# An attention-and-MLP kernel whose main loop is moved to row halves of the TensorE array

## The chip, the cores and the metric

The kernel runs on one core of a Trainium2 chip. The metric is device time in microseconds. Engines are named as in the profile: PE is TensorE (PEld its weight loads), DVE VectorE, ACT ScalarE, POOL GpSimd, SP SyncE, which issues the DMAs here.

## The reference, cut to what matters

```python
# q, k, v: (4, 12480, 128); agents: (4, 49, 128); w_in: (128, 2048); w_out: (2048, 128)
agent_v = softmax(agents @ k.T / sqrt(128)) @ v     # per batch, 49 x 128
x       = softmax(q @ agents.T / sqrt(128)) @ agent_v
h       = x @ w_in
g       = h - tanh(h)
out     = g @ w_out
```

All is float32. The kernel folds `agent_v @ w_in` into one matrix of 49 x 2048 per batch (`aw`), so that `h` is the product of the 49 softmax weights of a token with `aw`. The values of `h` are small, and `h - tanh(h)` is taken as h * tanh(sqrt(0.6) h)^2 / 1.8; a general path for larger values lies behind a branch that is not taken here.

## The kernel before

Tokens are worked on in blocks of 500 (25 per batch, 100 in all), the 2048 columns in 8 pairs of 128-column chunks. A step `(n, i)` is one block and one pair of chunks: 800 steps. Two blocks (16 steps) are a double block; `pos` is the step's place in it, 0 to 15. PE multiplies in one pass with a rounded type (`F32R`); to keep precision each operand is split into a high and a low part. A step does this:

- `first_product` / `m1`, two steps ahead: `h` = (`awh` + `awl`) times `pT`. `pT` has 98 rows: 49 of high parts and 49 of low ones, and `aw` stands twice above itself. So each chunk takes two matmuls, four per pair (L537, L538). `h` lies in two PSUM banks.
- `tanhs` and `squares` on ACT, one step ahead: `y` (L546), `z` (L551).
- `product` on DVE: `g` = h * z (L556, `mul`); then on POOL `gh` = `g` rounded (L589, `high`); then, a step later, DVE takes `gl` = g - gh (L594, `low`).
- `out` / `m2`: six matmuls per pair add `gh` and `gl` times the parts of `w_out` to `acc`, one PSUM bank (L606, L607, L609). In the pair `PLAIN_PAIR` (7) of every second block, and in the whole first block, `g` is not split: two f32 matmuls with `wo_f` take its place, which PE runs in two passes each (L603).

When a block is done, ACT copies `acc` into `o` with the scale `GSC` (L770), and SP writes two blocks at once (L773). Beside this, the generators in `live` advance once a step. `q_softmax` makes the weights of the next double block: 32 small matmuls in column quarters (L494), maximum, exponential, sum, then `pp`, high and low parts beside each other. `q_transpose` brings `pp` into `pT` by PE (L524) and a copy on ACT (L529). `phase1(b + 1)` does the softmax over k for the next batch: `scores` (L277), maxima, `av` (L336), and `project` makes its `aw`. In the last batch there is none of it. The PSUM has eight banks: the pool `ph` with three pairs (`h`), `pmisc` with two single ones for all else.

On each engine the order is the order in the code (`issue_order`); the tables `KS`, `VS`, `OS`, `T0`, `T1`, `QGAPS` say at which `pos` the side jobs start and how many steps lie between their parts.

Of the kernel before, what the change touches and what calls it, by code (L numbers as in the profile page):

```python
# [30 lines left out]
NCH = FF // 128  # L31
TT = 126
# [9 lines left out]
GW = 2 * BLK  # L42
NBLK = -(-N // BLK)
# [6 lines left out]
GSC = 1.0 / (3.0 * 0.6)  # L50
# [7 lines left out]
PLAIN_PAIR = NCH // 2 - 1  # L58
PLAIN_EVERY = 2
# [8 lines left out]
T0 = 12  # L68
T1 = 14
KS = (3, 5, 14)  # L70
VS = (1, 3, 12)
OS = (3, 5)
# [26 lines left out]
class Build:  # L99
    def __init__(self, ctx, tc, aps):  # L100
        self.tc, self.nc = tc, tc.nc
        self.qT, self.kT, self.v, self.agT, self.wi, self.wo, self.outT = aps
        self.pool = lambda name, bufs=1, **kw: tc.tile_pool(name=name, bufs=bufs, **kw)
        self.const = ctx.enter_context(self.pool("const"))
        self.keep = ctx.enter_context(self.pool("keep"))
        self.small = ctx.enter_context(self.pool("small", 2))
        self.ph = ctx.enter_context(self.pool("ph", 3, space=PSUM))
        self.pmisc = ctx.enter_context(self.pool("pmisc", 2, space=PSUM))
# [6 lines left out]

    def misc(self):
        return self.pmisc.tile([128, 512], F32, tag="misc", name="misc")

    def constants(self):
# [18 lines left out]
        self.wo_f = c.tile([128, 2, C], F32, tag="wo_f", name="wo_f")  # L138
        self.vb = [c.tile([128, GT, C + 2], F32, tag=f"v{i}", name=f"v{i}") for i in range(VB)]
        self.avs = c.tile([128, B, A2], F32, tag="avs", name="avs")  # L140
# [43 lines left out]
    def split_w_out(self, c):  # L184
# [7 lines left out]
        if c == PLAIN_PAIR // 2:  # L192
            nc.scalar.copy(self.wo_f.rearrange("p n e -> p (n e)"), w[:, 2 * C * (PLAIN_PAIR % 2) :][:, : 2 * C])

    def phase1(self, b):
# [36 lines left out]
        def scores(g):  # L232
            yield
            yield
# [8 lines left out]
            kt = ahead("k", load_k, g, 1 if b == 0 else kb - 1)  # L243
            if b and g >= NG - vb:
                ahead("v", load_v, 0, g - NG + vb + 1)
            if b == 0:
                ps = self.ph.tile([128, 2, 512], F32, tag="h", name="h")
# [65 lines left out]
        def av(g):  # L313
# [10 lines left out]
            yield  # L324
            if b:
                yield
                yield
            nc.scalar.activation(e3, e3, AF.Exp, scale=SCALE)
            yield
# [21 lines left out]
            if g == 0:  # L351
                ph = self.ph.tile([128, 2, 512], F32, tag="h", name="h")
                st["ps"], st["pr"] = ph[:, 0, :], ph[:, 1, :A]
# [33 lines left out]
        def sums():  # L387
# [6 lines left out]
            if b == 0:  # L394
# [8 lines left out]
                two = [128, 2, A]  # L403
                nc.vector.tensor_tensor(
                    self.avs[:, b, :].rearrange("p (two a) -> p two a", a=A),
                    pt[:, None, :A].broadcast_to(two),
                    sm[:, None, :].broadcast_to(two),
                    ALU.mult,
                )
# [11 lines left out]
            two = [128, 2, A]  # L421
            nc.vector.tensor_tensor(
                self.avs[:, b, :].rearrange("p (two a) -> p two a", a=A),
                pt[:, None, :A].broadcast_to(two),
                sm[:, None, :].broadcast_to(two),
                ALU.mult,
            )
# [5 lines left out]
        if b:  # L433
            jobs = [(KS, scores(g)) for g in range(NG)] + [(OS, max_in()), (OS, max_out())]
            jobs += [(VS, av(g)) for g in range(NG)]
            return jobs + [(OS, job) for job in [sums(), None] + self.project(b, True)]
# [3 lines left out]
    def project(self, b, bound):  # L440
        nc = self.nc

        def part(c, lo, hi):
            yield
            yield
            if c == 0:
                self.aw[b] = tuple(
# [4 lines left out]
            if b == 0 and bound and c < 2:  # L452
                ps = self.ph.tile([128, 2, 512], F32, tag="h", name="h")[:, 0, :]
            else:
                ps = self.misc()
            ps = ps[:A2, : hi - lo]
            nc.tensor.matmul(ps, self.avs[:, b, :], self.w_in[:, sl], start=True, stop=True)
            yield
            h = awh[:A2, sl]
# [3 lines left out]
            nc.vector.tensor_tensor(awl[:A2, sl], ps, h.bitcast(F32), ALU.subtract)  # L463
# [15 lines left out]
    def q_load(self, src):  # L479
        qt = self.keep.tile([128, GW], F32, tag="qt", name="qt", bufs=2)  # L480
# [3 lines left out]
    def q_softmax(self, halves, qt, res, TT=TT, gaps=(1,) * 7):  # L484
# [3 lines left out]
        for t in range(GT):  # L488
            b, at, w = halves[t // BT]
            at += min(t % BT * TT, w - TT)  # L490
            for r in range(0, TT, QUART):
                m = min(QUART, TT - r)
                to = ps[r : r + m, t * A : (t + 1) * A]
                nc.tensor.matmul(to, qt[:, at + r : at + r + m], self.ag[:, b, :], start=True, stop=True)  # L494
        yield from (None,) * gaps[1]
        pv = ps[:TT, : GT * A].rearrange("p (t a) -> p t a", a=A)
        m = self.small.tile([128, GT], F32, tag="qm", name="qm")
        e = self.small.tile([128, GT, A], F32, tag="qe", name="qe")
        ev = e[:TT]
        s = self.small.tile([128, GT], F32, tag="qs", name="qs")  # L500
        nc.vector.tensor_reduce(m[:TT], pv, axis=AX.X, op=ALU.max)
        nc.scalar.copy(ev, pv)  # L502
        yield from (None,) * gaps[2]
        nc.gpsimd.tensor_tensor(ev, ev, m[:TT, :, None].broadcast_to([TT, GT, A]), ALU.subtract)  # L504
# [3 lines left out]
        nc.vector.tensor_reduce(s[:TT], ev, axis=AX.X, op=ALU.add)  # L508
        nc.vector.tensor_scalar(s[:TT], s[:TT], EPS, None, ALU.add)
        nc.vector.reciprocal(s[:TT], s[:TT])  # L510
        nc.vector.tensor_tensor(ev, ev, s[:TT, :, None].broadcast_to([TT, GT, A]), ALU.mult)
        yield from (None,) * gaps[5]
        pp = self.small.tile([128, GT, A2], F32R, tag="pp", name="pp")
        (nc.scalar.copy if gaps[5] else nc.vector.tensor_copy)(pp[:TT, :, :A], ev)  # L514
        yield from (None,) * gaps[6]
        nc.gpsimd.tensor_tensor(pp[:TT, :, A:], ev, pp[:TT, :, :A].bitcast(F32), ALU.subtract)  # L516
        res.append(pp)

    def q_transpose(self, pp, half, res, w, TT=TT):
        nc = self.nc  # L520
        ps = self.misc()
        for t in range(BT):
            at = min(t * TT, w - TT)
            nc.tensor.transpose(  # L524
                ps[:A2, at : at + TT].bitcast(F32R), pp[:TT, half * BT + t, :], self.identr[:TT, :TT]
            )
        yield
        pT = self.keep.tile([128, BLK], F32R, tag="pT", name="pT", bufs=3)
        nc.scalar.copy(pT[:A2, :w], ps[:A2, :w])  # L529
        res.append(pT)  # L530

    def m1(self, aw, pT, i, w):
        nc = self.nc
        h = self.ph.tile([128, 2, 512], F32, tag="h", name="h")
        for c in range(2):
            sl = slice((2 * i + c) * 128, (2 * i + c + 1) * 128)
            nc.tensor.matmul(h[:, c, :w], aw[0][:A2, sl], pT[:A2, :w], start=True, stop=False)  # L537
            nc.tensor.matmul(h[:, c, :w], aw[1][:A2, sl], pT[:A2, :w], start=False, stop=True)  # L538
        return h[:, :, :w]

    def pair(self, t):
        return t.rearrange("p (c n) -> p c n", c=2)
# [6 lines left out]
    def square(self, y):  # L549
        z = self.wtile("z", NB["z"])[:, : y.shape[1]]  # L550
        self.nc.scalar.activation(z, y, AF.Square)  # L551
# [45 lines left out]
    def m2(self, acc, i, gh, gl, wf=None):  # L597
        nc = self.nc
        w = gh.shape[1] // 2
        parts = [(2 * i + c, slice(c * w, (c + 1) * w)) for c in range(2)]  # L600
        if gl is None:
            for c, (f, x) in enumerate(parts):
                nc.tensor.matmul(acc[:, :w], wf[:, c * C : (c + 1) * C], gh[:, x], start=f == 0, stop=f == NCH - 1)  # L603
            return
        for f, x in parts:
            nc.tensor.matmul(acc[:, :w], self.wo_l[:, f, :], gh[:, x], start=f == 0, stop=False)  # L606
            nc.tensor.matmul(acc[:, :w], self.wo_h[:, f, :], gh[:, x], start=False, stop=False)  # L607
        for f, x in parts:
# [326 lines left out]
```

## Time and profile before

| | |
|---|---|
| median of 3 runs | 2103.64 us (2102.35 to 2104.73) |
| the profiled execution | 2104.99 us, of it 2102.9 us span |
| granted TensorE clock | 0.996 |
| PE busy | 2072.6 us |
| DVE busy | 1958.9 us |
| ACT busy | 1796.8 us |
| POOL busy | 1409.8 us |
| first `g` of the main loop | at 60.12 us |

Busy time is the union of the recorded durations of an engine. Durations overlap where an engine pipelines: consecutive matmuls are recorded with 0.39 us each though they start 0.23 us apart, and a DVE operation of 1.19 us is followed after 1.11 us. Distances between starts therefore say what an operation occupies.

### The profile page before, as it was taken

What the parts mean: (1) busy time and instruction counts of PE and PEld (TensorE: products, weight loads), DVE (VectorE), ACT (ScalarE), POOL (GpSimd) and SP (SyncE); (2) the same over time, 40 slices, a digit from 0 to 9 for tenths busy, and PEclk for the clock granted to TensorE, in tenths of its full rate; (3) what the DMA queues carried; (4) which work ended last, traced back from release to release, by engine and by line L of the source; (5) the groups of instructions that cost most, each with busy time, mean ns of one, the idle gap of its engine ahead of it and who ended that gap; (6) DMA issues with size and microseconds to landing.
All of it is one profiled execution on the core that took longest, in us unless ns stands there. A gap on an engine that the chain in (4) does not pass through costs nothing.

```text
span 2102.9 us, 37664 instructions
## 1 busy us (share of the span) xinstructions
PE 2072.6 (99%) x14885; PEld 1642.1 (78%) x14885; DVE 1958.9 (93%) x2076; ACT 1796.8 (85%) x2088; POOL 1409.8 (67%) x857
## 2 busy tenths in 40 slices
PE   8899999999999999999999999999999999999998
PEld 7577777777777777877777777777777878878876
DVE  7899999999999999989999999999999999999998
ACT  3788889988888888998888888889888888888887
POOL 0366676667767676666677677667667777777776
PEclk9999999999999999999999999999999999999999
DMA  9222102210111121112002210121100000100000
GB/s 338 98 61 80 54 31 71 70 52 30 40 51 50 54 70 50 50 62 60 21 20 71 70 33 30 50 61 42 34 27 20 30 30 20 40 20 21 30 11 21
DMA packets 65353, 109.17 MB, mean 52 GB/s; under 512 B 3984, under 2 KB 44176, under 8 KB 65168
## 3 DMA queue, kind: packets, MB, share of 16 engines
q1 hardware_dynamic: 65168, 106.68, 15.5%
q8 instruction: 119, 1.95, 0.4%
q14 instruction: 66, 0.54, 0.1%
HBM read 81.10 MB, written 25.56 MB: 51 GB/s over the span
## 4 chain that ended last, share of the span: by engine, by line
PE 83%; DVE 11%; ACT 3%; issue 2%; POOL 1%; DMA 0%; POOLq 0%; SPq 0%; DVEq 0%; ACTq 0%
PE h L537 16%; PE h L538 15%; PE misc L609 15%; PE misc L606 14%; PE misc L607 14%; DVE g L556 4%; DVE gl L594 3%; PE misc L603 2%; PE misc L336 2%; PE misc L494 2%; PE h L249 1%; PE misc L524 1%; PE misc L277 1%; ACT z L551 1%; ACT y L546 1%
## 5 line engine op out<-in xcount | busy, mean ns | idle before, releaser
L589 POOL TENSOR_SCALAR gh<-g 128x1000 fp32r<-128x1000 f32 (+1 forms) x704 | 1230.8, 1748 | 347.0 <-DVE g L556 337.0
L556 DVE TENSOR_TENSOR g<-h,z 128x1000 f32<-128x1000 f32 (+1 forms) x800 | 951.2, 1192 | 102.3 <-ACT z L551 98.5
L546 ACT ACTIVATE y<-h 128x1000 f32<-128x1000 f32 (+1 forms) x800 | 805.0, 1006 | 225.9 <-PE h L538 220.5
L594 DVE TENSOR_TENSOR gl<-g,gh 128x1000 fp32r<-128x1000 f32 (+1 forms) x743 | 887.3, 1194 | 7.5 <-POOL gh L589 1.8
L551 ACT ACTIVATE z<-y 128x1000 f32<-128x1000 f32 (+1 forms) x800 | 833.8, 1042 | 17.5 <-DVE g L556 2.3
L537 PE MATMUL h<-pT,awh 98*128 98x500 f32 (+1 forms) x1600 | 668.7, 418 | 2.1 <-ACT awh L460 1.4
L538 PE MATMUL h<-pT,awl 98*128 98x500 f32 (+1 forms) x1600 | 622.3, 389 | 0.5 <-DVE awl L463 0.5
L606 PE MATMUL misc<-gh,wo_l 128*128 128x500 f32 (+1 forms) x1486 | 576.6, 388 | 0.5 <-POOL gh L589 0.5
L607 PE MATMUL misc<-gh,wo_h 128*128 128x500 f32 (+1 forms) x1486 | 575.0, 387 | 0.0
L609 PE MATMUL misc<-gl,wo_h 128*128 128x500 f32 (+1 forms) x1486 | 461.1, 391 | 10.8 <-DVE gl L594 9.5
L537 PEld LDWEIGHTS h<-pT,awh 98*128 98x128 f32 x1600 | 300.3, 188 | 85.8 <-issue 18.1
L538 PEld LDWEIGHTS h<-pT,awl 98*128 98x128 f32 x1600 | 302.2, 189 | 65.8 <-issue 13.6
L609 PEld LDWEIGHTS misc<-gl,wo_h 128*128 128x128 f32 x1486 | 274.0, 188 | 81.4 <-DVE gl L594 29.8
L606 PEld LDWEIGHTS misc<-gh,wo_l 128*128 128x128 f32 x1486 | 279.7, 188 | 59.7 <-POOL gh L589 3.3
L607 PEld LDWEIGHTS misc<-gh,wo_h 128*128 128x128 f32 x1486 | 280.8, 189 | 55.3
L516 POOL TENSOR_TENSOR pp<-qe,pp 126x392 fp32r<-126x392 f32 x50 | 49.1, 982 | 199.7 <-DVE pp L514 192.2
L504 POOL TENSOR_TENSOR qe<-qe,qm 126x392 f32<-126x392 f32 x50 | 55.2, 1105 | 111.5 <-ACT qe L502 111.5
L603 PE MATMUL misc<-g,wo_f 128*128 128x500 f32 (+1 forms) x196 | 90.1, 581 | 0.0
L321 POOL TENSOR_TENSOR s<-s,mb 128x392 f32<-128x392 f32 (+1 forms) x39 | 70.3, 1801 | 26.1 <-DVE g L556 26.1
L770 ACT ACTIVATE o<-misc 128x500 f32<-128x500 f32 (+1 forms) x100 | 58.0, 580 | 5.3 <-PE misc L609 5.3
L529 ACT CAST pT<-misc 98x500 fp32r<-98x500 f32 (+1 forms) x100 | 56.6, 567 | 1.8 <-PE misc L524 1.8
L603 PEld LDWEIGHTS misc<-g,wo_f 128*128 128x128 f32 x196 | 37.0, 189 | 26.3 <-issue 22.6
(105 smaller groups left out, 840.1 us busy)
## 6 DMA issues: line engine op xcount, KB each, us to landing
kt<-kT SPq DMA_DIRECT2D x48, 512.0 KB, 3.7
qt<-qT SPq DMA_DIRECT2D x46, 500.0 KB, 3.5
outT<-o SPq DMA_DIRECT2D x46, 500.0 KB, 2.6
v<-v SPq DMA_DIRECT2D x36, 512.0 KB, 4.1
vt<-v SPq DMA_DIRECT2D x12, 512.0 KB, 6.4
raw<-w_in SPq DMA_DIRECT2D x4, 512.0 KB, 9.3
v<-w_out SPq DMA_DIRECT2D x4, 512.0 KB, 8.2
qt<-qT SPq DMA_DIRECT2D x4, 490.0 KB, 3.4
```

The lines of the kernel that those rows point to most:

```text
L321: (nc.gpsimd if b else nc.vector).tensor_tensor(e3, sv, top, ALU.subtract)
L537: nc.tensor.matmul(h[:, c, :w], aw[0][:A2, sl], pT[:A2, :w], start=True, stop=False)
L538: nc.tensor.matmul(h[:, c, :w], aw[1][:A2, sl], pT[:A2, :w], start=False, stop=True)
L546: self.nc.scalar.activation(self.pair(y), h, AF.Tanh, scale=TSC)
L551: self.nc.scalar.activation(z, y, AF.Square)
L556: self.nc.vector.tensor_tensor(self.pair(g), h, self.pair(z), ALU.mult)
L589: self.nc.gpsimd.tensor_scalar(gh, g, 1.0, 0.0, ALU.mult, ALU.add)
L594: self.nc.vector.tensor_tensor(gl, g, gh.bitcast(F32), ALU.subtract)
L603: nc.tensor.matmul(acc[:, :w], wf[:, c * C : (c + 1) * C], gh[:, x], start=f == 0, stop=f == NCH - 1)
L606: nc.tensor.matmul(acc[:, :w], self.wo_l[:, f, :], gh[:, x], start=f == 0, stop=False)
L607: nc.tensor.matmul(acc[:, :w], self.wo_h[:, f, :], gh[:, x], start=False, stop=False)
L609: nc.tensor.matmul(acc[:, :w], self.wo_h[:, f, :], gl[:, x], start=False, stop=f == NCH - 1)
```

## The change

1. The array is used in two row halves. `aw` and `pT` stand at rows 0 to 48 and 64 to 112; a second tile `pb` holds `pT` with its parts exchanged, made by two DMAs. `m1` takes three products per chunk (low x high, high x high, high x low) of 49 rows each; the two chunks of a pair use the two halves, alternating, and two banks. Six half matmuls take the place of four whole ones.
2. `m2` takes each of its products in two halves of 64 rows, which add up in two banks of `acc`: twelve half matmuls for six. At a block's end ACT copies the one bank (`take`), and DVE adds the other (`add_up`). The scale goes into the Square of `z`.
3. f32 pairs stand at positions 3, 7 and 15 of a double block (`PLAIN`), where there was one at 7. (The short title of the change speaks of four; the code has three.)
4. One PSUM pool of four pairs of banks serves `h`, `acc`, the transposes (`pt`) and `misc`; two side jobs of one step can share a pair (`share`). In a step where a pair was lent out, and at `i == 2`, `first_product` stands behind `product` (`late`).
5. Transposes are half matmuls; tokens of a block are cut at 125 with halves of 63 and 62 that overlap, `h` has 504 columns, of which 500 are read. `pp` is one tile for all double blocks. The side jobs' positions are new.

```diff
-PLAIN_PAIR = NCH // 2 - 1
-PLAIN_EVERY = 2
+PLAIN = (3, 7, 15)
...
-T0 = 12
-T1 = 14
-KS = (3, 5, 14)
-VS = (1, 3, 12)
-OS = (3, 5)
+T0 = 11
+T1 = 15
+KS = {2: 1, 12: 2}
+VS = {15: 1, 9: 1, 11: 1}
+VGAPS = {15: (3, 1), 9: (3, 2), 11: (2, 1)}
+OS = {3: 1, 5: 1}
...
-        self.ph = ctx.enter_context(self.pool("ph", 3, space=PSUM))
-        self.pmisc = ctx.enter_context(self.pool("pmisc", 2, space=PSUM))
+        self.ph = ctx.enter_context(self.pool("ph", 4, space=PSUM))
...
+    def banks(self, name):
+        self.taken += 1
+        return self.ph.tile([128, 2, 512], F32, tag="h", name=name)
+
     def misc(self):
-        return self.pmisc.tile([128, 512], F32, tag="misc", name="misc")
+        if self.spare is not None:
+            ps, self.spare = self.spare, None
+            return ps
+        t = self.banks("misc")
+        if self.sharing:
+            self.spare = t[:, 1, :]
+        return t[:, 0, :]
...
+        pT, pb = (self.keep.tile([128, BT * TT], F32R, tag=t, name=t, bufs=2) for t in ("pT", "pb"))
...
+        nc.sync.dma_start(pb[HALF:PW].bitcast(F32), pT[:A].bitcast(F32))
+        nc.sync.dma_start(pb[:A].bitcast(F32), pT[HALF:PW].bitcast(F32))
...
     def m1(self, aw, pT, i, w):
+        h = self.banks("h")
+        rows = slice(0, A), slice(HALF, PW)
+        terms = (((1, 0), (0, 0)), ((0, 0), (1, 1)), ((0, 1), (0, 1)))
+        for k, both in enumerate(terms):
+            for c, (a, p) in enumerate(both):
+                sl = slice((2 * i + c) * 128, (2 * i + c + 1) * 128)
+                nc.tensor.matmul(
+                    h[:, c, : BT * TT], aw[a][rows[c], sl], pT[p][rows[c], :], start=k == 0, stop=k == 2
+                )
...
     def m2(self, acc, i, gh, gl, wf=None):
+            terms = [(low, gh, 0), (high, gh, 0), (low, gh, 1), (high, gh, 1), (high, gl, 0), (high, gl, 1)]
+        for k, (weights, g, c) in enumerate(terms):
+            for r in range(2):
+                rows = slice(HALF * r, HALF * (r + 1))
+                nc.tensor.matmul(
+                    acc[:, r, :w],
+                    weights(c)[rows],
+                    g[rows, c * w : (c + 1) * w],
...
+    def add_up(self, o, acc):
+        self.nc.vector.tensor_tensor(o, o, acc[:, 1, : o.shape[1]], ALU.add)
+
+    def take(self, o, acc):
+        self.nc.scalar.copy(o, acc[:, 0, : o.shape[1]])
...
             squares(k + 1)
-            first_product(k + AHEAD)
+            late = self.taken > taken or n and i == 2
+            if not late:
+                first_product(k + AHEAD)
...
             product(k, values)
+            if late:
+                first_product(k + AHEAD)
+            while done and done[0][1] < k - 1:
+                finish(done.pop(0)[0])
             low(1)
```

On PE, an f32 pair and the step after it in the last batch, before:

```order
L603 MATMUL misc<-g,wo_f 128x500 x2
L537 MATMUL h<-pT,awh 128x500
L538 MATMUL h<-pT,awl 128x500
L537 MATMUL h<-pT,awh 128x500
L538 MATMUL h<-pT,awl 128x500
L606 MATMUL misc<-gh,wo_l 128x500
L607 MATMUL misc<-gh,wo_h 128x500
L606 MATMUL misc<-gh,wo_l 128x500
L607 MATMUL misc<-gh,wo_h 128x500
L609 MATMUL misc<-gl,wo_h 128x500 x2
```

The same place now, `wo_f_86` being the f32 weights of one plain pair:

```order
L635 MATMUL acc<-g,wo_f_86 128x500 x4
L563 MATMUL h<-pT,awl 128x504
L563 MATMUL h<-pT,awh 128x504 x2
L563 MATMUL h<-pb,awl 128x504
L563 MATMUL h<-pb,awh 128x504 x2
L635 MATMUL acc<-gh,wo_l 128x500 x2
L635 MATMUL acc<-gh,wo_h 128x500 x2
L635 MATMUL acc<-gh,wo_l 128x500 x2
L635 MATMUL acc<-gh,wo_h 128x500 x2
L635 MATMUL acc<-gl,wo_h 128x500 x4
```

Six half matmuls stand for four whole ones in `m1`, twelve for six in `m2`, and every two neighbours use different halves.

On DVE, the steps around the maximum of the q scores (`qm`), early in a double block of the last batch, before:

```order
L556 TENSOR_TENSOR g<-h,z 128x1000
L594 TENSOR_TENSOR gl<-g,gh 128x1000
L556 TENSOR_TENSOR g<-h,z 128x1000
L594 TENSOR_TENSOR gl<-g,gh 128x1000
L501 TENSOR_REDUCE qm<-misc 126x8
L556 TENSOR_TENSOR g<-h,z 128x1000
L594 TENSOR_TENSOR gl<-g,gh 128x1000
```

And now:

```order
L583 TENSOR_TENSOR g<-h,z 128x1000
L644 TENSOR_TENSOR o<-o,acc 128x500
L621 TENSOR_TENSOR gl<-g,gh 128x1000
L583 TENSOR_TENSOR g<-h,z 128x1000
L621 TENSOR_TENSOR gl<-g,gh 128x1000
L514 TENSOR_REDUCE qm<-misc 128x8
L583 TENSOR_TENSOR g<-h,z 128x1000 x2
L621 TENSOR_TENSOR gl<-g,gh 128x1000
```

`add_up` (L644) has come in between `g` and `gl`, and the f32 pair at position 3 leaves two `g` in a row.

On SP, one double block of the last batch, before:

```order
L773 DMA outT<-o 128x1000
L481 DMA qt<-qT 128x1000
L773 DMA outT<-o 128x1000
L481 DMA qt<-qT 128x1000
L773 DMA outT<-o 128x1000
```

And now:

```order
L812 DMA outT<-o 128x1000
L495 DMA qt_98<-qT 128x1000
L551 DMA pb<-pT 49x504
L552 DMA pb<-pT 49x504
L551 DMA pb<-pT 49x504
L552 DMA pb<-pT 49x504
L812 DMA outT<-o 128x1000
```

Four transfers per double block have come in, each behind the copy of `pT` on ACT.

More of the change, by code (lines that the diff above doesn't have):

```diff
@@ L31 @@
 NCH = FF // 128
+PW = HALF + A
 TT = 126
@@ L42 @@
 GW = 2 * BLK
+QW = GW + 8
+TS = 128
 NBLK = -(-N // BLK)
@@ L806, in out @@
                 if i == 0:
-                    acc[n] = self.misc()
-                wf = self.wf[:, 2 * C * i :] if n == 0 else self.wo_f.rearrange("p c n -> p (c n)")
+                    acc[n] = self.banks("acc")
+                wf = self.wf[:, 2 * C * i :] if n == 0 else self.wo_f.get(i)
                 self.m2(acc[n], i, gh, gl, wf)
@@ L834, in fast @@
             nxt = []
+            taken = self.taken
+            self.share(True)
             for gen in live:
@@ L870, in fast @@
         while done:
+            self.take(out_at(done[0][0]), acc[done[0][0]])
             finish(done.pop(0)[0])
```

207 lines of the change are left out of this document (105 added, 102 removed).

## The prediction

> **What bounds the kernel now.** I read the page's busy times first, then the same by stage, then the chain and the waits, and last the timeline of one stretch. The busy times:
>
> ```profile
> PE 2072.6 (99%) x14885; PEld 1642.1 (78%) x14885; DVE 1958.9 (93%) x2076; ACT 1796.8 (85%) x2088; POOL 1409.8 (67%) x857
> PE 83%; DVE 11%; ACT 3%; issue 2%; POOL 1%; DMA 0%; POOLq 0%; SPq 0%; DVEq 0%; ACTq 0%
> ```
>
> The second line is the chain that ended last: PE holds 83% of it. The output transfers mark the double blocks (two blocks, 16 steps), one each:
>
> ```profile
> 157.07 0.34 SPq L773 DMA_DIRECT2D outT<-o  x1
> ...
> 1640.27 0.34 SPq L773 DMA_DIRECT2D outT<-o  x1
> ...
> 1948.20 0.34 SPq L773 DMA_DIRECT2D outT<-o  x1
> 157.07:1640.27 1483.20, 1475.69 (x11011) 1168.45 (x11010) 1385.85 (x1453) 1290.55 (x1494) 1017.41 (x613) 1.00 0.15 48
> 1640.27:2063.60 423.33, 423.12 (x2532) 339.09 (x2531) 408.65 (x408) 377.86 (x419) 313.74 (x188) 1.00 0.07 25
> ```
>
> There are 36 double blocks between the first two transfers, 41.20 us each: they carry the next batch's softmax over k beside their own work (stage A). After that there is none of it, and eight take 307.93, 38.49 us each (stage B, 11 of them to 2063.6). The last two rows are busy time by stage, in the order PE, PEld, DVE, ACT, POOL. PE is busy throughout; DVE has 38.50 us of work per double block in A and 37.15 in B, ACT 35.85 and 34.35. So PE bounds both stages and DVE is only 1.3 to 2.7 us behind. The waits say the same from the other side:
>
> ```profile
> ACT y L546 <- PE h L538: 220.5, 397, 1.5
> DVE g L556 <- ACT z L551: 98.5, 214, 0.9
> ```
>
> ACT waits for PE's `h`, DVE for ACT. The span in parts is 157.07 + 36 x 41.20 + 11 x 38.49 + 39.3 = 2103. The profiled execution took 2104.99 around a span of 2102.9; the median of the runs is 2103.64, so I add 0.7 to a span to speak of the median.
>
> **One step on PE and on DVE.** Busy PE is not yet PE at its peak, so I take the distance between starts:
>
> ```profile
> 1902.54 0.39 PE L537 MATMUL h<-pT,awh 98*128 98x500 f32 x1
> 1902.77 0.39 PE L538 MATMUL h<-pT,awl 98*128 98x500 f32 x1
> ...
> 1903.23 0.39 PE L538 MATMUL h<-pT,awl 98*128 98x500 f32 x1
> ...
> 1904.81 0.39 PE L537 MATMUL h<-pT,awh 98*128 98x500 f32 x1
> 1904.95 1.19 DVE L594 TENSOR_TENSOR gl<-g,gh 128x1000 fp32r<-128x1000 f32 x1
> 1906.06 1.19 DVE L556 TENSOR_TENSOR g<-h,z 128x1000 f32<-128x1000 f32 x1
> 1907.17 1.19 DVE L594 TENSOR_TENSOR gl<-g,gh 128x1000 fp32r<-128x1000 f32 x1
> 1908.28 1.20 DVE L556 TENSOR_TENSOR g<-h,z 128x1000 f32<-128x1000 f32 x1
> ```
>
> Ten matmuls from 1902.54 to 1904.81: 0.227 us a slot, 2.27 a step. DVE does a step's two operations in 2.22, with no gap. An ordinary step is therefore nearly balanced already; what is worth most is whatever relieves both engines.
>
> **The change, part by part.**
>
> *`h` in three products per pair.* Four slots become three if the two half-array matmuls of a pair run side by side. 16 steps x 0.227 = -3.63 us per double block on PE. The second product `m2` keeps six slots, as twelve halves in pairs. No row of the trace shows row halves. The nearest are the column quarters of the q scores:
>
> ```profile
> 1911.16 0.62 PE L609 MATMUL misc<-gl,wo_h 128*128 128x500 f32 x2
> 1911.70 0.90 PE L494 MATMUL misc<-ag,qt 128*32 128x49 f32 x64
> 1912.53 0.50 PE L537 MATMUL h<-pT,awh 98*128 98x500 f32 x1
> ```
>
> 64 passes of 49 columns took 0.83 us. A plain f32 pass of 500 columns takes 0.42 (next rows), so 64 such passes one after another would take 64 x 49 x 0.84 ns = 2.6 us: they overlapped 3.2-fold out of 4, including what one start costs. Bounds for a slot of two halves: below, 0.21 (half of that 0.42, the bare streaming of 500 columns); above, 0.227 / (3.2/4) = 0.284. I take 0.227, since 500 columns hide far more of a start than 49 do, and keep both ends. The weight loads double: 18 per step. The transposes show 62 ns for a load and a matmul with 98 weight columns (four in 0.25 us), so 81 ns for 128 columns and 162 for two, under 0.227.
>
> ```profile
> 1899.97 0.41 PE L524 MATMUL misc<-identr,pp 126*98 126x126 f32 x4
> 1900.22 0.46 PE L537 MATMUL h<-pT,awh 98*128 98x500 f32 x1
> ```
>
> The Trainium skill ("TensorE: Matmul & The Clock Gate", Part 3, "Measured speedup vs the span model") gives a pack of tiles the time of one matmul plus about 4 ns for each further tile; by that a slot is 0.231, and 126 slots a double block add 0.5 us to each, some 20 us to the sum below.
>
> *More f32 pairs: three per double block instead of one* (positions 3, 7 and 15). The price on PE:
>
> ```profile
> 1000.51 1.84 PE L603 MATMUL misc<-g,wo_f 128*128 128x500 f32 x4
> 1001.80 0.78 PE L537 MATMUL h<-pT,awh 98*128 98x500 f32 x1
> 1002.41 0.39 PE L538 MATMUL h<-pT,awl 98*128 98x500 f32 x1
> ```
>
> From 1000.51 to 1002.41 stand four f32 passes and one slot: 1.67 for the pair against 1.36 for six slots, +0.31, twice: +0.62. (As halves the passes of one half follow each other; if the halves overlap less, up to twice that.) Each saves DVE a `gl`: -2 x 1.11. It also saves POOL a `gh`. After a plain pair DVE has only a `g` between a `g` and its `gl`, so it could wait for POOL:
>
> ```profile
> 1926.19 1.03 POOL L589 TENSOR_SCALAR gh<-g 128x1000 fp32r<-128x1000 f32 x1 [0.22 <-DVE g L556]
> 1924.84 2.30 DVE L556 TENSOR_TENSOR g<-h,z 128x1000 f32<-128x1000 f32 x2
> 1927.25 1.20 DVE L594 TENSOR_TENSOR gl<-g,gh 128x1000 fp32r<-128x1000 f32 x1
> ```
>
> There the `gh` took 1.03 and the `gl` started on time: no new wait, 0 (at worst 0.8, if `gh` takes the 1.84 us that it has beside a `gl`).
>
> *Output in two banks.* `take` on ACT stands for the old copy (L770), at the same length. `add_up` is a new DVE operation, two per double block, half as wide as a `g`: 0.55 each, +1.1. Its own row is missing; the ends are 0.4 (a 392-wide `qm` occupies 0.48) and 0.7.
>
> *Transposes* become eight half ones per block, 0.13 to 0.5 against 0.25 now: 0. The scale moves into the Square: 0. Splitting into `h` of stride 126 inside the tiles: 0, ACT and DVE read as many elements; at worst a few per cent. Memsets at the start lie on POOL, which is idle there.
>
> *The PSUM pool.* Eight banks were three `h` pairs and two singles; now they are four pairs for all. While a pair is lent to scores, transposes or a second `acc`, `h` has two, and the first product moves behind the step's `g` (positions 2, 3, 10, 11, 15, and 13 or 14 in stage A). Then m1 for step k+2 waits for `g` of step k, and what follows must fit into the time in which DVE does three operations, 3.33 us. The links:
>
> ```profile
> 1901.39 1.01 ACT L546 ACTIVATE y<-h 128x1000 f32<-128x1000 f32 x1 [0.47 <-PE h L538]
> 1902.30 0.57 ACT L529 CAST pT<-misc 98x500 fp32r<-98x500 f32 x1
> 1902.75 1.05 ACT L551 ACTIVATE z<-y 128x1000 f32<-128x1000 f32 x1
> 1903.69 1.01 ACT L546 ACTIVATE y<-h 128x1000 f32<-128x1000 f32 x1
> 1904.74 1.04 ACT L551 ACTIVATE z<-y 128x1000 f32<-128x1000 f32 x1
> ```
>
> From the first m1 (1902.54) to `y` (1903.69) it is 1.15, 0.92 with a slot less; `y` and `z` end 2.09 later; three handovers of 0.07: 3.2, which fits. Behind positions 11 and 15 the copy of `pT` lies between `y` and `z`, 0.45 more: 3.66, 0.33 too late, twice. With an exponential there as well in part of stage A I take 0.8 us of DVE waiting per double block; the ends are 0 and 3 (0.5 at each of six places). Behind the waiting m1 PE holds `m2` of step k-1, which needs `gl` of that step, later anyway.
>
> *Two transfers per block on SP* copy `pT` into `pb`, behind the copy on ACT. Only the first block's are near: between the copy and the m1 that needs them lie a `z` (1.04), a `g` (1.2), a `gl` (1.1) and two slots, 3.9 us.
>
> ```profile
> outT<-o SPq DMA_DIRECT2D x46, 500.0 KB, 2.6
> kt<-kT SPq DMA_DIRECT2D x48, 512.0 KB, 3.7
> ```
>
> With 0.34 to issue each and 2.6 to land it is 3.3: covered by 0.6. If that cover goes, PE waits in m1's last product.
>
> **The sum.** PE: -3.63 + 0.62 = -3.0: 38.2 in A, 35.5 in B. DVE: -2.22 + 1.1 = -1.1: 37.4 and 36.05. ACT stays at 35.85 and 34.35. So PE still bounds A at 38.2, DVE bounds B at 36.05; with 0.8 of waiting 39.0 and 36.85. Ahead of 157 us two double blocks gain about 4 together, the end 1.7. Sum: 153 + 36 x 39.0 + 11 x 36.85 + 37.6 = 2000.0, a gain of 103; 2001 in terms of the median.
>
> **The rivals.**
>
> *A: waits eat half of it.* If `pb` lands as slowly as the k loads (3.7 + 0.7) PE waits 0.5 per double block, 47 x 0.5 = 24: 2025; if the two transfers land one after the other, 2 us: 2095. For it: the two waits above already add up to 319 us. Against: the transfers are a fifth of the size of `outT`.
>
> *B: the pair of halves costs more than a slot: slower.* The gain of 103 is 2.2 us in each of 47 double blocks, spread over 126 slots: 0.0175. From 0.245 us per pair the kernel is slower. At the upper bound of 0.284 it is 47 x (126 x 0.057 - 0.3) = +324: 2325. For it: 0.227 against the 0.21 of bare streaming shows a cost of 17 ns per matmul, and if each half pays it in turn, the pair stands at 0.244. Against: the 64 quarter passes above, each with its own weight load, took 0.83 us, 13 ns each, so no such cost is paid by every instruction in turn. The same page of the Trainium skill lists four row tiles of 32 rows at 3.07 times the speed of one; taken over to two halves that makes a slot 0.295 and the time about 2390; no run here shows it yet.
>
> *C: nothing waits.* A slot at 0.21, no losses: DVE bounds both stages, 36 x 37.4 + 11 x 36.05 + 189 = 1932.
>
> *D: the halves don't overlap at all*, so the change does not do what it says: 126 x 0.454 + 3 x 3.34 + 2.0 = 69 per double block, about 3630. Against it: the overlap of the quarters.
>
> **How the numbers follow.** My forecast has 63% (1955 to 2050), A 14%, C 8%, B 11%, D 2%; 2% for a result within 0.2%, which is about what a measurement of this kernel can tell from no change. Faster: 63 + 14 + 8 = 85%; slower: 13%. The range reaches from C to a slot of 0.24 (A 40.8, B 38.1 us: 2082): 1935 to 2085. It leaves out B, D and little else.
>
> **What would show it.** Right: the page has PE's share falling, starts of the two halves of a pair a few ns apart and pairs 0.227 apart; transfers of output 39 and 36.9 us apart; ACT waits for PE less than 220 us; DVE's busy time at about 1905. Wrong: pairs over 0.24 apart; a long wait of `h` for a DMA of `pb`; a `g` that waits for `z` more than before, at positions 12 and 0 above all; `gl` waiting for `gh` after plain pairs.

## The result: slower, and the profile after

The changed kernel takes 2240.8 us (2236.36 to 2242.15) against 2103.0 for the kernel before, a ratio of 1.065, interval 1.063 to 1.067. The forecast was 2001 us. The granted TensorE clock was 0.991 to 0.992 against 0.996 in the profiled run before; if all of that were lost time, it would be some 11 of the 138 us. The page's busy times and chain, which answer to the first two lines of the prediction:

```profile
PE 2066.6 (92%) x21175; PEld 1487.1 (67%) x21175; DVE 1957.1 (88%) x2085; ACT 1786.9 (80%) x2077; POOL 1104.5 (49%) x774
PE 38%; DVE 33%; ACT 14%; issue 12%; POOL 2%; DMA 0%; DVEq 0%; SPq 0%; ACTq 0%; POOLq 0%
```

No engine is full any more: PE's share of the chain fell from 83% to 38%, and the rest goes round by DVE and ACT. The output transfers from the timeline, and busy time by stage (PE, PEld, DVE, ACT, POOL):

```profile
162.94 0.35 SPq L812 DMA_DIRECT2D outT<-o  x1
...
1752.33 0.35 SPq L812 DMA_DIRECT2D outT<-o  x1
...
2194.25 0.34 SPq L812 DMA_DIRECT2D outT<-o  x1
162.94:1752.33 1589.39, 1472.87 (x15485) 1057.74 (x15483) 1387.74 (x1458) 1283.21 (x1481) 795.09 (x553) 0.99 0.17 54
1752.33:2194.25 441.92, 423.86 (x3920) 304.87 (x3918) 405.61 (x408) 373.61 (x419) 241.81 (x166) 1.00 0.10 34
```

A double block of stage A takes 1589.39 / 36 = 44.15 us, one of stage B 441.92 / 11 = 40.17 (before 41.20 and 38.49). DVE's busy time is 38.55 and 36.87, so it idles 5.6 and 3.3 (before 2.7 and 1.3). From PE's timeline, a whole `m2` and the `m1` behind it:

```profile
2003.80 0.42 PE L635 MATMUL acc<-gh,wo_l 64*128 64x500 f32 x2
2004.03 0.42 PE L635 MATMUL acc<-gh,wo_h 64*128 64x500 f32 x2
2004.26 0.41 PE L635 MATMUL acc<-gh,wo_l 64*128 64x500 f32 x2
2004.48 0.42 PE L635 MATMUL acc<-gh,wo_h 64*128 64x500 f32 x2
2004.71 0.64 PE L635 MATMUL acc<-gl,wo_h 64*128 64x500 f32 x4
2005.16 0.39 PE L563 MATMUL h<-pT,awl 49*128 49x504 f32 x1
...
2005.85 0.42 PE L635 MATMUL acc<-gh,wo_l 64*128 64x500 f32 x2
```

Two halves are merged in each of the first four rows, four in the fifth. A pair of halves takes 0.22 to 0.23 us, in `m2` and in the three pairs of `m1` (0.69 from 2005.16 to 2005.85): the halves overlap as forecast. So PE has less to do and still the kernel is slower. PE's busy time hardly fell, because it counts the recorded length of a matmul, which reaches over short gaps. The waits of DVE and ACT:

```profile
DVE g L583 <- ACT z L578: 125.2, 173, 2.1
DVE s L304 <- ACT s L310: 22.1, 12, 2.7
DVE s L304 <- ACT qe L515: 21.9, 13, 1.7
DVE acc L370 <- ACT qe L515: 20.6, 12, 1.7
DVE o L644 <- ACT o L647: 19.2, 41, 2.2
ACT y L573 <- PE h L563: 332.2, 331, 2.5
```

`g` waits for `z` in fewer cases than before (214 then) but longer, up to 2.1 us where 0.9 was the most. The next four rows are new. `s` and `acc` of the softmax over k wait for ACT reads of another job, 64.6 us in three rows; by the code (`share`) the two jobs stand in one PSUM pair, and `e9` sets them apart.

Two places of stage B explain most of the rest. First DVE and POOL at the end of a block:

```profile
1891.54 1.19 DVE L583 TENSOR_TENSOR g<-h,z 128x1000 f32<-128x1000 f32 x1
1892.65 0.67 DVE L644 TENSOR_TENSOR o<-o,acc 128x500 f32<-128x500 f32 x1
1892.89 1.03 POOL L616 TENSOR_SCALAR gh<-g 128x1000 fp32r<-128x1000 f32 x1 [0.38 <-DVE g L583]
1893.23 1.73 DVE L621 TENSOR_TENSOR gl<-g,gh 128x1000 fp32r<-128x1000 f32 x1
```

Ordinarily `gl` starts right behind `g`, ahead of the next `gh`. With `add_up` (L644) between, POOL's `gh` starts first, and `gl` takes 1.73 instead of 1.19: it ends 1.04 after the end of `gh`, as if it had begun only then. The Trainium skill ("SBUF — State Buffer", "SBUF: two separate sides") says that a DVE operation with two SBUF inputs and a reading GpSimd operation exclude each other, and that the one which starts first holds the port for the whole instruction; these rows agree.

Second, a round with a late first product (a round goes from `g(k)` over the first product, `y` and `z` to `g(k+2)`), from DVE, PE and ACT in turn:

```profile
1904.02 1.19 DVE L583 TENSOR_TENSOR g<-h,z 128x1000 f32<-128x1000 f32 x1
1905.26 0.49 PE L563 MATMUL h<-pT,awl 49*128 49x504 f32 x1
1906.26 1.01 ACT L573 ACTIVATE y<-h 128x1000 f32<-128x1000 f32 x1 [0.71 <-PE h L563]
1907.16 0.58 ACT L547 CAST pT<-pt 113x504 fp32r<-113x504 f32 x1
1907.62 1.05 ACT L578 ACTIVATE z<-y 128x1000 f32<-128x1000 f32 x1
1908.71 1.20 DVE L583 TENSOR_TENSOR g<-h,z 128x1000 f32<-128x1000 f32 x1 [1.28 <-ACT z L578]
```

From `g(k)` over m1, `y`, the copy of `pT` and `z` to `g(k+2)` it is 4.69 us, 4.2 without the copy. Two ordinary steps of DVE are 4.44. But here pair 15 is an f32 pair, so one `gl` is missing, DVE has 3.33 of work, and waits 1.28.

### The profile page after: what moved, and what is told of

The parts are those of the page before. It is cut to its first block, busy times and chain, and to the rows that moved or that the text cites. A ratio compares the mean times of both kernels' runs of the same rounds, so it can differ in the third digit from the quotient of the medians.

```text
span 2234.3 us, 50723 instructions
## 1 busy us (share of the span) xinstructions
PE 2066.6 (92%) x21175; PEld 1487.1 (67%) x21175; DVE 1957.1 (88%) x2085; ACT 1786.9 (80%) x2077; POOL 1104.5 (49%) x774
## 4 chain that ended last, share of the span: by engine, by line
PE 38%; DVE 33%; ACT 14%; issue 12%; POOL 2%; DMA 0%; DVEq 0%; SPq 0%; ACTq 0%; POOLq 0%
PE acc L635 17%; PE h L563 14%; DVE g L583 14%; DVE gl L621 13%; ACT z L578 5%; ACT y L573 3%; ACT o L647 2%; PE misc L508 2%; PE misc L358 2%; DVE o L644 1%; DVE qe L524 1%; PE misc L302 1%; ACT qe L519 1%; PE h L274 1%; DVE qs L521 1%
## 5 line engine op out<-in xcount | busy, mean ns | idle before, releaser
L616 POOL TENSOR_SCALAR gh<-g 128x1000 fp32r<-128x1000 f32 (+1 forms) x617 | 945.4, 1532 | 575.0 <-DVE g L583 568.8
L583 DVE TENSOR_TENSOR g<-h,z 128x1000 f32<-128x1000 f32 (+1 forms) x800 | 947.8, 1190 | 127.7 <-ACT z L578 125.2
L563 PE MATMUL h<-pT,awh 49*128 49x504 f32 x1600 | 586.1, 448 | 0.4 <-issue 0.4
L635 PE MATMUL acc<-gh,wo_l 64*128 64x500 f32 (+1 forms) x2576 | 518.3, 390 | 10.3 <-POOL gh L616 9.0
L635 PE MATMUL acc<-gh,wo_h 64*128 64x500 f32 (+1 forms) x2576 | 514.0, 386 | 0.0
L563 PE MATMUL h<-pT,awl 49*128 49x504 f32 x800 | 404.0, 505 | 87.4 <-DVE g L583 38.9
L635 PE MATMUL acc<-gl,wo_h 64*128 64x500 f32 (+1 forms) x2576 | 423.3, 402 | 50.3 <-DVE gl L621 47.7
L563 PE MATMUL h<-pb,awh 49*128 49x504 f32 x1600 | 321.0, 389 | 0.4 <-DMA pb<-pT 0.4
L563 PE MATMUL h<-pb,awl 49*128 49x504 f32 x800 | 311.1, 389 | 0.5 <-issue 0.5
L563 PEld LDWEIGHTS h<-pT,awh 49*128 49x128 f32 x1600 | 260.3, 187 | 29.7 <-issue 24.4
L635 PE MATMUL acc<-g,wo_f 64*128 64x500 f32 (+1 forms) x1184 | 280.0, 589 | 0.0
```

Of the source, the lines that this page charges most:

```text
L563: nc.tensor.matmul(h[:, c, : BT * TT], aw[a][rows[c], sl], pT[p][rows[c], :], start=k == 0, stop=k == 2)
L583: self.nc.vector.tensor_tensor(self.pair(g), h, self.pair(z), ALU.mult)
L616: self.nc.gpsimd.tensor_scalar(gh, g, 1.0, 0.0, ALU.mult, ALU.add)
L635: nc.tensor.matmul(acc[:, r, :w], weights(c)[rows], g[rows, c * w : (c + 1) * w], start=i == 0 and k == 0, stop=i == NCH // 2 - 1 and k == ...
```

## The experiments

Idle time and the stretching of `gl` (what it takes beyond 1.19 us) are means per double block, added up from the DVE rows of each trace; a position here is the step from one `g` to the next. `e1` to `e4` and `e6` to `e8` were executed once each, the others two to five times.

**add_up behind gl** (`e4`), against the stretched `gl`:

```diff
-            while done and done[0][1] < k - 1:
-                finish(done.pop(0)[0])
             low(1)
+            while done and done[0][1] < k - 1:
+                finish(done.pop(0)[0])
```

> The changed kernel with add_up (and the output's DMA) behind gl of the same step instead of ahead of it. Theory 1 (with add_up in between, POOL starts gh before DVE starts gl, and gl is held up until gh is done: 0.55 and 0.24 us longer in stage B, 0.4 and 0.3 in stage A, and so much of DVE's path): gl back at 1.19 us everywhere, 0.8 us in each double block, 2200 us. Theory 2 (DVE has idle time enough and the longer gl is not on the path): gl at 1.19, but the time within 10 us of 2241.

2184.6 us, 56 less, theory 1 and 15 us beyond its number. DVE's timeline with the `gh` of POOL:

```profile
1849.78 1.19 DVE L621 TENSOR_TENSOR gl<-g,gh 128x1000 fp32r<-128x1000 f32 x1
1850.02 1.86 POOL L616 TENSOR_SCALAR gh<-g 128x1000 fp32r<-128x1000 f32 x1 [0.38 <-DVE g L583]
1850.89 0.67 DVE L644 TENSOR_TENSOR o<-o,acc 128x500 f32<-128x500 f32 x1
1851.47 1.19 DVE L583 TENSOR_TENSOR g<-h,z 128x1000 f32<-128x1000 f32 x1
```

The lengthening fell from 0.77 to 0 per double block in B and from 0.97 to 0.26 in A, and `add_up`'s own wait for ACT from 19.2 to 3.9 us. The first is about 34 us (36 x 0.71 + 11 x 0.77), the second 15, together most of the 56. `add_up` itself occupies 0.58.

**No two side jobs in one pair** (`e9`, on top of the last; the jobs move to other steps for it):

```diff
-KS = {2: 1, 12: 2}
-VGAPS = {15: (3, 1), 9: (3, 2), 11: (2, 1)}
+KS = {5: 1, 8: 1, 13: 1}
+VGAPS = {15: (3, 2), 9: (3, 1), 11: (2, 1)}
```

> The changed kernel with add_up behind gl, and with the side jobs set one step apart so that no two of them share a pair of PSUM banks. Theory 1 (a DVE reader of a side job waits for the other job's ACT reader because both stand in one pair; these waits are some 64 us of DVE idle, nearly all in stage A): from 2185 us to 2120 to 2135, the rows 's <- ACT s', 's <- ACT qe', 'acc <- ACT qe' gone, stage A's double block from 43.15 to 41.5. Theory 2 (the lent pair itself, and the late step it makes, is the loss, so that as many or more pairs lent cost as much): 2175 to 2200, the same idle time named after other tiles.

2155.0 us: 30 less, half way between the two. The three waits of `s` and `acc` for ACT are gone, but `g` waits for `z` 166.5 us (127.1 in `e4`): of 64 us, some 39 moved to there. Whether the sharing made these waits or the steps of the jobs, this run doesn't tell apart. In stage B, where the softmax over k is done, a double block took 39.08 us in both runs.

**The places of the f32 pairs.** First in the changed kernel, one pair only (`e2`) and three others (`e3`):

```diff
-PLAIN = (3, 7, 15)
+PLAIN = (7,)          # e2
+PLAIN = (0, 5, 8)     # e3
```

> The changed kernel with f32 pairs at position 7 alone. Theory 1 (the pairs at 3 and 15 save DVE a gl just where g of a late step waits for z, so that the saved 2.2 us came back as waits of 1.28 and 1.09 us): the two gl fill the waits, the time stays within 15 us of 2241. Theory 2 (DVE's work sets the pace and the saving is real): 49 x 2.2 = 108 us more, 2350 us. If PE set the pace, 49 x 0.62 = 30 us less, 2210.

> The changed kernel with the three f32 pairs at positions 0, 5 and 8, away from the late steps and the steps just ahead of them. Theory 1 (as for the run with one f32 pair): the saving of two gl is kept, the waits at positions 0 and 4 fall from 1.28 and 1.09 to under 0.4: about 1.8 us in each of 49 double blocks, 2150 us. Theory 2 (the waits of g for z come from ACT and PE wherever the f32 pairs stand): within 15 us of 2241.

`e2`: 2281.0, +40, none of the numbers expected; `e3`: 2240.5, theory 2. Without the pairs 3 and 15 `g` waits for `z` 36.4 us instead of 125.2: two `gl` more a double block are 47 x 2.22 = 104 us of work, and 89 come back as less waiting (`gl` was stretched more instead, 1.85 in B against 0.77). At 3 and 15 the two pairs were thus worth 40 us of the 104. At 0, 5 and 8 the idle moved along, to positions 1, 5, 6 and 10 (at 10 as a wait of `add_up` for ACT, 56.6 us in all). Their missing `gl` belong to steps 1, 6 and 9, outside the rounds of the places 2, 3, 10, 11 and 15, and still they were worth no more: leaving those rounds alone is not enough. Then on top of `e9` (`e12`, `e13`, `e17`), and in the changed kernel with no other edit (`e16`):

```diff
-PLAIN = (3, 7, 15)
+PLAIN = (6, 7)          # e12
+PLAIN = (2, 6, 7)       # e13, e16
+PLAIN = (2, 6, 7, 10)   # e17
```

> The changed kernel with add_up behind gl and no shared pairs, with two f32 pairs at positions 6 and 7 in place of three at 3, 7 and 15. Theory 1 (a missing gl leaves DVE short of work, since ACT needs 2.05 us for tanh and square of the next step, and is kept only where DVE has other work: step 7 with the query softmax takes 4.14 us; the idle of 1.28 and 1.00 behind the pairs 15 and 3 is their saving lost): work +1.11, idle -2.3 to -2.6 a double block, so 41.0 in stage A, 38.0 in stage B, and 2155 - 36 x 1.45 - 11 x 1.08 = 2091 us. Theory 2 (the idle at those places belongs to the late products and stays): one gl more to do, +1.11 x 47 = 2207 us.

> As the one with f32 pairs 6 and 7, and a third one at position 2, whose missing gl falls in step 3 (DVE has 0.47 us of other work there). Theory 1: some 0.5 us of its 1.11 is kept, 0.6 turns to idle: 2091 - 47 x 0.5 = 2068 us, idle at position 3 about 0.6. Theory 2 (the place of the f32 pairs doesn't matter, three are three): 2155 us give or take 10.

> The changed kernel as it is (add_up ahead of gl, shared pairs) with the f32 pairs at 2, 6 and 7 alone. Theory 1 (the places of the f32 pairs are worth what they were beside the other two edits, 61 us): 2240 - 61 = 2180 us. Theory 2 (the gain needs the other two: behind add_up and the shared pairs the DVE waits elsewhere instead, as when the pairs were moved to 0, 5 and 8): 2220 to 2245 us.

> As the fastest so far (add_up behind gl, no shared pairs, f32 pairs 2, 6 and 7), with a fourth f32 pair at position 10, whose missing gl falls in step 11 behind add_up's step. Theory 1 (a missing gl is kept only so far as DVE has other work in the step; there is none in step 11 of stage B): 0.3 to 0.6 of its 1.11 us kept, 2094 - 47 x 0.45 = 2073 us. Theory 2 (PE, with 0.31 more a double block, and the idle take it all): 2094 to 2110 us.

`e12` 2136.1, `e13` 2094.0, `e16` 2171.7, `e17` 2095.7. `e12` does one `gl` more than `e9` and is 19 us faster; it missed its 2091, in part because a `gl` in step 5 now waited for `gh` (22.4 us, and 0.8 of stretching there in B, 0.5 in A). `e13`, 61 below `e9`, is the fastest, though short of its 2068: ratio to the kernel before 0.9951, interval 0.9935 to 0.9968. Its busy times, and by stage:

```profile
PE 2006.0 (96%) x21179; PEld 1521.1 (73%) x21179; DVE 1922.1 (92%) x2086; ACT 1793.7 (86%) x2090; POOL 1179.5 (56%) x763
159.96:1636.76 1476.80, 1430.36 (x15483) 1083.14 (x15482) 1359.30 (x1458) 1289.01 (x1493) 841.96 (x540) 1.00 0.18 58
1636.76:2054.11 417.35, 407.50 (x3918) 307.07 (x3916) 398.01 (x408) 374.94 (x419) 265.06 (x165) 1.00 0.11 36
```

41.02 and 37.94 a double block; idle is down to 3.3 and 1.8 (4.8 and 3.1 in `e9`). The `gl` of pairs 6 and 7 are missing in steps 7 and 8, and in step 7 DVE has 1.9 us of the query softmax to do; the rounds behind 15 and 3 have their `gl` again. The `gl` of pair 2 is missing in step 3, beside 0.57 us of other work, and 0.48 of idle stands there. `e16` shows that the places work without the other edits: -69. The granted clock differs too: `e9` took 2150.0 us at 0.991 and 2157.3 at 0.986 and 0.987, so an estimated 10 of the 61 us may be the clock, 0.994 to 0.997 in `e13`. The same may hold for a like part of the 69 (0.995 to 0.997 in `e16`, 0.991 and 0.992 in the changed kernel). `e17` shows the limit. DVE's rows:

```profile
1808.54 1.20 DVE L583 TENSOR_TENSOR g<-h,z 128x1000 f32<-128x1000 f32 x1
1810.09 1.20 DVE L583 TENSOR_TENSOR g<-h,z 128x1000 f32<-128x1000 f32 x1 [0.36 <-ACT z L578]
1811.21 1.19 DVE L621 TENSOR_TENSOR gl<-g,gh 128x1000 fp32r<-128x1000 f32 x1
1813.22 1.20 DVE L583 TENSOR_TENSOR g<-h,z 128x1000 f32<-128x1000 f32 x1 [0.82 <-ACT z L578]
```

The saved 1.11 came back as 0.36 and 0.82 of waiting (0 and 0.18 in `e13`) in steps 11 and 12, where the late rounds of 10 and 11 end.

**The loop without side work**, before (`e10`) and after (`e11`): softmax and values of batches 1 to 3 and the later query softmax and transposes are left out.

```diff
-                kq = self.phase1(b + 1)
...
-            if p + 1 < npair and pos in (T0, T1):
+            if p == 0 and pos in (T0, T1):
...
-            if p and p + 1 < npair:
+            if False:
```

> The kernel before, with the side work of the main loop left out: batches 1 to 3's scores, softmax and values aren't made (all batches use the first one's aw), nor the query softmax and its transposes beyond the second double block (pT of that block is used on). What is left is the loop of h, tanh, square, g, gh, gl, the sum for the output, and its transfer. All theories: PE-bound, 16 times 10 slots of 0.227 us less the f32 pair's 2 slots plus its 0.31 = 36.2 us a double block, up to 36.8 with the DMAs' changes; 49 of them and the start: 1860 to 1900 us.

> The changed kernel with the same side work left out as in the kernel before without side work. Theory 1 (the loop itself got shorter, and the loss comes from side jobs taking a pair of the four PSUM pairs): DVE-bound, 29 x 1.11 + 2 x 0.59 and a late step or two, 33.5 to 34.5 us a double block, 1730 to 1790 us, 80 us or more below the bare kernel before. Theory 2 (the loop in halves on four pairs waits by itself, by add_up ahead of gl and the long chain g, y, z): no shorter than 36 us a double block, at or above the bare kernel before.

1907.6 and 1893.8. `e10` lies 8 us above its range, though 36.57 a double block is inside. Of `e11`, theory 1 missed; theory 2 had the double block right (no shorter than 36) but not the total, which is below `e10`. 47 double blocks, before first:

```profile
148.45:1867.10 1718.65, 1718.65 (x7428) 1401.43 (x7427) 1629.13 (x1458) 1565.90 (x1599) 1264.35 (x706) 1.00 0.04 15
```

```profile
152.63:1852.92 1700.29, 1663.18 (x12976) 1220.97 (x12974) 1592.65 (x1458) 1558.70 (x1599) 935.86 (x611) 1.00 0.04 15
```

36.57 against 36.18 us: even bare, the loop gains 0.4. DVE's work fell to 33.9, but it idles 2.3, 1.3 of it in the steps behind f32 pairs (positions 0, 4 and 8), where DVE has only 1.11 us of work and ACT needs 2.05 a step for `y` and `z`, and 0.9 in the steps with `add_up` (2 and 10).

**Late products alone.** In the kernel before, behind `g` at positions 2, 3, 10, 11 and 15 (`e1`), and there made to wait for `g` by an added dependency (`e8`):

```diff
-            first_product(k + AHEAD)
+            late = n and pos in (2, 3, 10, 11, 15)
+            if not late:
+                first_product(k + AHEAD)
...
             product(k, values)
+            if late:
+                first = self.count()
+                first_product(k + AHEAD)
+                self.wait_for(first, self.mul_at)
```

> The kernel before, with one thing changed: at positions 2, 3, 10, 11 and 15 (from the second block on) the first product of step k+2 stands behind the product of step k, as in the changed kernel; PSUM, halves and f32 pairs stay as before. Theory 1 (the order of the late steps is what costs: m1 waits for g of step k, and y, z and g of step k+2 hang on it): m1 takes 1.15 us up to the start of y here, y and z 2.09, handovers 0.2, so 3.4 to 3.9 us against 3.33 of DVE work in between, and PE, which bounds this kernel, stands still meanwhile, 0.3 to 0.8 us at each of five places: 1.5 to 4 us in each of 49 double blocks, 2175 to 2300 us. Theory 2 (the order costs nothing as long as h has three pairs; the loss of the changed kernel comes from its DVE work and the f32 pairs): within 0.5% of 2103 us.

> The kernel before, in which the first product of step k+2 waits for g of step k at positions 2, 3, 10, 11 and 15, by an added dependency (the earlier run with the changed order alone left PE's order and waits as they were, since h had three pairs). Theory 1 (this wait is what the changed kernel lost its time to): 3.4 to 3.9 us of chain against 3.33, and PE stands still while it bounds: 1.5 to 4 us per double block, 2175 to 2300 us. Theory 2 (the wait is mostly hidden, and sharing a PSUM pair, add_up and the longer gl took the time): under 0.5 us per double block, below 2130 us.

`e1`: 2103.4, nothing; three `h` pairs leave the late product nothing to wait for, so it tested only the order. `e8`: 2147.8, +45, between the two numbers. In the changed loop without side work the wait stood at 5, 6, 12, 13 and 14 (`e15`; the same without the added wait, `e14`, left the order on the engines as in `e11`, and took 1894.8 us), then at 3, 7 and 15, the f32 pairs' steps (`e18`):

```diff
-            late = self.taken > taken or n and i == 2
+            late = n and (i == 2 or pos in (5, 6, 12, 13, 14))   # e14, e15
+            late = n and (i == 2 or pos in (3, 7, 15))           # e18
```

> The changed kernel without side work (the same work left out as in the other bare kernels), and at positions 5, 6, 12, 13 and 14 the first product of h really waits for g, by an added dependency. Moving its place alone had given the same program, so that run said nothing. Theory L (the late product is a price of its own in this loop: 1.36 us of products, 1.0 tanh, 1.04 square against 3.33 us of DVE work): 0.2 to 0.4 a late step, 36.17 + 1.0 to 2.0 a double block, 1942 to 1990 us, the idle in the steps behind those positions. Theory R (late products are taken up by the slack between PE and DVE, and cost only beside side work or f32 pairs): 1890 to 1915 us.

> The changed kernel without side work (the same work left out as in the other bare kernels), with the first product of h made to wait for g at positions 3, 7 and 15, the f32 pairs' own steps, in place of 5, 6, 12, 13 and 14. From g(k) over a late product, tanh and square to g(k+2) the rows of the other runs give 4.36 us; DVE has 4.44 of work in two ordinary steps, 3.33 where an f32 pair's gl is missing, which at these three positions is always so. Theory 1 (a late product costs only where a gl is missing from its round): up to 1.03 idle at each of the three, against 0.29, 0.69 and 0.29 there without, +1.2 to 1.8 us a double block, 1950 to 1985 us, more for three late steps than the 19 us of five. Theory 2 (late steps all cost alike, 0.08 us as in that run): 1900 to 1910 us.

`e15`: 1913.1, +19 for five late steps (theory R); the added idle stands at step 0 alone, behind the f32 pair 15 (0.78 against 0.29). `e18`: 1958.8, +65 for three (theory 1). Its round, from DVE's timeline:

```profile
1804.33 1.19 DVE L583 TENSOR_TENSOR g<-h,z 128x1000 f32<-128x1000 f32 x1
1805.43 1.18 DVE L621 TENSOR_TENSOR gl<-g,gh 128x1000 fp32r<-128x1000 f32 x1
1806.54 1.19 DVE L583 TENSOR_TENSOR g<-h,z 128x1000 f32<-128x1000 f32 x1
1808.67 1.20 DVE L583 TENSOR_TENSOR g<-h,z 128x1000 f32<-128x1000 f32 x1 [0.94 <-ACT z L578]
```

The round takes 4.34 us, which 4.44 of DVE work hides and 3.33 doesn't. A late product alone added 0.08 us on the mean (`e15`), a missing `gl` alone left 0.3 to 0.7 of idle (`e11`); in one round they leave 0.95.

**Three products or f32 pairs alone.** m1 in halves with `m2` whole and the old PSUM pools and f32 pair (`e5`), with three f32 pairs (`e6`); the kernel before with those three (`e7`).

```diff
-PLAIN_PAIR = NCH // 2 - 1
-PLAIN_EVERY = 2
+PLAIN = (7,)          # e5
+PLAIN = (3, 7, 15)    # e6, e7
...
     def m1(self, aw, pT, i, w):   # e5, e6: as in the changed kernel, m2 as before
```

> The kernel before with one part of the change: h in three half products per chunk (with pb and its DMAs, the first block's transposes one step earlier). m2 on the whole array, one bank for acc, the old PSUM pools, one f32 pair, no add_up, no late step. Theory 1 (the halves pay, and what lost the time is the PSUM pool, the late steps and add_up): PE falls by 3.63 us per double block to 37.6 and 34.9, DVE (38.5 and 37.15) bounds both stages: 153 + 36 x 39.0 + 11 x 37.4 + 38 = about 2006 us. Theory 2 (a change between halves and the whole array costs as much as that between the whole array and quarters, 0.095 us by the distance 0.32 instead of 0.227; two a step, 3.0 us per double block): PE 40.6 and 37.9, about 2076 us. Theory 3 (a change costs 0.2 us): 6.4 us per double block, about 2240.

> As the run with three products alone, with f32 pairs at positions 3, 7 and 15. Theory 1: DVE falls by 2.2 us to 36.3 and 34.9, PE stands at 38.2 and 35.5: about 1975 us. Theory 2 (a change of the array's use costs 0.095): PE 41.2 and 38.5, about 2100 us, slower than without the f32 pairs.

> The kernel before with f32 pairs at positions 3, 7 and 15 instead of one at 7; nothing else. Theory 1 (PE sets the pace of the kernel before, an f32 pair costs it 0.31 us): 49 x 0.62 = 30 us more, 2133 us. Theory 2 (DVE's work is on the path as well): the 2.2 us that it saves outweigh this, 2060 us.

`e5` took 2206.5 (ratio 1.049, interval 1.047 to 1.051), nearest to theory 3 and its 2240; `e6` 2236.2, where both theories missed; `e7` 2130.7, theory 1. In `e5` PE is full again, with three slots instead of four:

```profile
1800.29 0.49 PE L545 MATMUL h<-pT,awl 49*128 49x504 f32 x1
...
1800.63 0.39 PE L545 MATMUL h<-pb,awl 49*128 49x504 f32 x1
...
1800.86 0.39 PE L545 MATMUL h<-pb,awh 49*128 49x504 f32 x2
1801.18 0.49 PE L615 MATMUL misc<-gh,wo_l 128*128 128x500 f32 x1
1801.51 0.39 PE L616 MATMUL misc<-gh,wo_h 128*128 128x500 f32 x1
1801.73 0.39 PE L615 MATMUL misc<-gh,wo_l 128*128 128x500 f32 x1
```

At the change from halves to the whole array the distances are 0.32 and 0.33 instead of 0.23, and likewise back: 0.2 us a change, two a step, more than the slot saved. The double blocks, 43.15 and 40.95 us against 37.6 and 34.9 without any such cost, give 0.17 and 0.19 a change. The Trainium skill ("TensorEngine Tiling (Array Packing)", "Key Properties") says that a change of tiling mode drains TensorE; in this trace the change costs 0.2 us. So in this kernel three products pay only with `m2` in halves too, and `add_up` comes with the second bank. `e6` is 30 above `e5`, `e7` 28 above the kernel before: two more f32 pairs at 0.31 on a full PE (47 x 0.62 = 29).

## Why the prediction was wrong, by its steps

What failed is the step from less work to less time: the prediction let DVE's work (37.4 and 36.05) and PE's bound the double block with 0.8 us of waiting. The work came out nearly so; the waiting did not.

- **`h` in three products**: right. Pairs are 0.227 apart, so rivals B and D are out (D's "about 3630" is nearer 3550 by its own 69 us a double block). The Trainium skill ("TensorE: Matmul & The Clock Gate", Part 3, "Measured speedup vs the span model") would by estimate have a slot 4 ns longer, 0.231, by its cost per tile, and 0.295 by its 3.07 for four tiles carried over to two: the measured 0.227 is near the one and bears out nothing of the other.
- **f32 pairs**: PE's price right (`e6`, `e7`), "-2 x 1.11" on DVE the step that failed most. The work was saved, 104 us, but only 40 of it in time (`e2`), because the two `gl` were taken out of rounds in which DVE had too little else to do: late ones (`e18`), but others as well (`e3`, `e11`). Putting them at 2, 6 and 7, two of them beside the query softmax, gave 61 us (`e9` to `e13`) and 69 us (`e16`).
- **The PSUM pool**: the links were right (3.2 us from the end of `g(k)`; 4.34 - 1.11 = 3.2 measured), but the comparison was with three DVE operations, 3.33, at all places; behind pairs 3 and 15 there are two, 2.22. The text named both the late places 3 and 15 and the f32 pairs 3 and 15, and did not lay them on one another. Nor did it count the jobs that share a pair (30 us by `e9`). Of the two places that it named for a longer wait of `g`, 0 came (1.28 us in B, 1.47 in A) and 12 hardly (0.18 and 0.33); step 4, behind the f32 pair 3 (1.09 in B), it did not name. The idle in the forecast, 0.8 us per double block in B and 1.6 in A, became 3.3 and 5.6.
- **`add_up`**: 0.55 forecast, 0.58 measured; the term left out was what it does to the `gl` behind it: 0.97 a double block in A, 0.77 in B. Both ends of 0.4 and 0.7 missed that, since they priced the operation and not its place. Putting it behind `gl` gave 56 us (`e4`), some 34 of it in `gl` and 15 in `add_up`'s wait for ACT.
- **`pb` and transposes**: right; PE waited 0.4 us in all for `pb`. The worry about `gl` after plain pairs did not come true there.
- **The sum**: DVE's work without the stretched `gl` came out at 37.6 and 36.1, forecast 37.4 and 36.05. All of the miss is in how it fits together: against 39.0 in A, idle beyond the forecast's 1.6 is +4.0, stretched `gl` +1.0, work +0.2; in B against 36.85 +2.5, +0.8 and 0.05. That is 36 x 5.15 + 11 x 3.3 = 222 us, and 12 at start and end; the median lies 6.5 above the span, where 0.7 was added. The slower outcome was given to a PE that got dearer (B); it came instead from waits between DVE, ACT and PE, with no engine full.

With the three causes mended (`e13`) 93 us over the forecast remain. The loop as changed gains only 14 us bare, not 100, so much of it is missing without any side work. What is left in stage A, 3.3 us of idle spread over more than ten positions with at most 0.6 at one, was not taken apart; its cause stays open.

## What to carry to other kernels

Work taken off an engine is gain only where the round that feeds it is shorter than what is left: lay every place where a buffer's wait gets longer over every place where its cover gets shorter. Price a new operation at its place in the queue, with what it lets another engine start first. When two engines are within a few per cent of each other, taking work off both can leave the dependencies between them as the bound, as here, so compare the round, not the sums.

## What the runs showed of the hardware

- Half the array's rows at a time cost nothing in the slot: two halves of 49 or 64 rows and 504 or 500 columns stood at 0.227, as one matmul of the whole array. Going between halves and whole cost 0.2 us each time (`e5`).
- An operation of 0.58 us on DVE cost another 0.54 (position 10 in B; 0.23 at position 2) in the `gl` behind it, because it let POOL start first; with the order turned it cost nothing there (`e4`). Beside a `gl` that starts first it is `gh` that takes 1.85 instead of 1.03.
